# First batch of an attention and feed-forward kernel: scaling diagonals on GpSimd, value products on column halves, x split over all partitions

## The chip, the cores and the metric

The kernel runs on one core of one Trainium2 chip. A core has a matrix engine (TensorE, PE in the profile; its weight loads are listed apart as PEld), a vector engine (VectorE, DVE), a scalar engine (ScalarE, ACT), a general engine (GpSimd, POOL) and a queue engine that issues most transfers (SyncE, SP). The metric is device microseconds of one execution; the kernel before takes 1075.93 us (median of three runs, 1074.74 to 1076.09). A difference below about 0.2% can't be told from no change here.

## The reference

Eight batches of eight heads. Each head has 512 local rows and 32 global rows of 64 numbers. A local row attends to the 32 global keys and to the local keys no further than 32 rows away; a global row attends to everything. The concatenated heads (x, 512 wide, 544 rows a batch) go through a feed-forward layer.

```python
s_ll = np.where(np.abs(pos[:, None] - pos[None, :]) <= 32, scale * q_l @ k_l.T, -1e9)
s_l = np.concatenate([scale * q_l @ k_g.T, s_ll], axis=-1)
out_l = sm(s_l) @ np.concatenate([v_g, v_l])          # local rows
out_g = sm(scale * q_g @ k_all.T) @ v_all             # global rows
h = x @ w_in                                          # 512 x 2048
out = (np.maximum(h, 0) + np.log1p(np.exp(-abs(h)))) @ w_out
```

## The kernel before

Heads are taken in pairs: pair m is two heads of one batch, one on partitions 0 to 63 and one on 64 to 127. Pairs 0 to 3 are the first batch. They have code of their own (functions ending in 0), because nothing else can be done before x of the first batch is there. All later pairs run as small pieces (`scores`, `maxima`, `probs`, `values`, `combine`, `invert`, `normalise`) between the products of the feed-forward layer, which starts with batch 0.

The first batch is cut into eight local units (m, a), each two blocks of 128 query rows of both heads, so four row blocks a unit, and two global units (`scores0g` and so on), of two pairs each. A unit goes through seven stages, all in fp32:

- `scores0`: TensorE adds the mask and the products of queries and keys into PSUM (tile s, line 126 like every matmul); `soft0` takes the row maximum (VectorE, line 164), scales it (line 165), and ScalarE takes four exponentials with their sums (line 167).
- `invert0`: VectorE adds a small number to the sums and inverts them (lines 173 and 174).
- `diag0`: ScalarE multiplies the identity by the inverses, 128x128 for each of the four row blocks (line 181, tile diag). There are two diag tiles in turn.
- `turn0`: TensorE multiplies the exponentials by these diagonals, which transposes and normalises them in one step (tile t).
- `evict0`: ScalarE (line 208) and VectorE (line 209) copy t out of PSUM.
- `values0`: TensorE multiplies the values by them (tile o). Before, the stationary operand is 128 columns wide: both heads' values, so each product gives both heads' outputs against both heads' probabilities, and only the matching quarter blocks are used.
- `split0`: x is kept as a high part xh (ScalarE, line 226) and the remainder xl (VectorE, line 228), once for each head since the two heads' outputs stand in different columns.

The order is written out: a loop over k runs `scores0` of unit k + 2, the splitting of one weight block, `invert0` of unit k + 2, `values0` and `split0` of unit k - 2, `turn0` and `evict0` of unit k, and `diag0` of unit k + 2. Splitting a weight block takes, on each pass, one absolute value on ScalarE (line 479), four VectorE operations (lines 486, 488, 489, 492), a ScalarE cast (line 497) and a GpSimd subtraction (line 498). The helper `keep` ties each engine's operations of this part to that order. `diag0` comes before lines 497 and 479 on ScalarE. When the last units run, the pieces of pairs 4 and 5 begin, and after them the feed-forward products of batch 0 (tile h, then o from wo) with the remaining weight blocks; there no order is tied, and the scheduler's timeline sets each engine's order.

In each pass the later work of batch 0 needs xh and xl of all four pairs; the last is the xl of unit (3, 1). The global unit n = 1 has its scores in the PSUM tile oB, which the scores of unit (3, 1) used before it, so it waits for their exponentials.

Of the kernel before, what the change touches and what calls it, by code (L numbers as in the profile page):

```python
# [8 lines left out]
F32 = mybir.dt.float32  # L9
# [4 lines left out]
ALU = mybir.AluOpType  # L14
# [5 lines left out]
P = 128  # L20
# [33 lines left out]
def moe_over_global_local_attention(  # L54
# [12 lines left out]
    nc = tc.nc  # L67
# [3 lines left out]
    ps_h = ctx.enter_context(tc.tile_pool(name="ps_h", bufs=2, space=PSUM))  # L71
# [11 lines left out]
    identf = pl.tile([P, P], F32, tag="e", name="identf", bufs=2)  # L83
# [7 lines left out]
    for o, w, base, sign in ((32, 32, 0, 1), (64, 32, -96, -1), (96, 128, 32, 1), (96, 128, 32, -1)):  # L91
        r = mask0[:, 0, 1, o:o + w]
# [26 lines left out]
    def after(i, what):  # L119

        if what in order:
            tc.add_manual_dep(i.ins, order[what].name, mybir.DependencyInfo(mybir.DependencyClass.NoSync, mybir.DependencyReason.DATA), reason="order")
        return i

    def mm(*a, **k):
        order["pe"] = after(nc.tensor.matmul(*a, **k), "pe").ins  # L126
# [3 lines left out]
    st = {}  # L130
# [4 lines left out]
    xh, xl = {}, {}  # L135
# [14 lines left out]
    def keep(what, i):  # L150
        order[what] = after(i, what).ins
# [24 lines left out]
    def diag0(name, n):  # L176

        t = st.pop(("sums", name))
        d = st["diag", name] = pl.tile([P, 4, P], F32, tag="s2", name=f"diag{name}", bufs=2)
        for i in range(n):  # L180
            keep("act", nc.scalar.mul(d[:, i], identf, t[:, 0, i:i + 1]))

    def scores0(m, a):
        raw = st["raw0", m, a]
# [25 lines left out]

    def values0(m, a):
        t, vt = st.pop(("p0", m, a)), st["v0", m]
        ps = st["o0", m, a] = ps_h.tile([P, 512], F32, tag="h", name=f"o0_{m}_{a}").rearrange("p (c h q) -> p c h q", c=2, h=2)
        for c in range(2):
            for k, n in enumerate((P, 96)):
                mm(ps[:, c], lhsT=vt[:n, 2 * a + c, k], rhs=t[k][:n, :, c], start=k == 0, stop=k == 1, skip_group_check=True)

    def split0(m, a):
        ps = st.pop(("o0", m, a))
        if a == 0:  # L220
            xh[m] = pl.tile([P, 512], F32R, tag=f"xh{m}", name=f"xh0_{m}", bufs=1)
            xl[m] = pl.tile([P, 512], F32R, tag=f"xl{m}", name=f"xl0_{m}", bufs=1)
        hi, lo = ([x[m][r, 256 * a:256 * a + 256].rearrange("p (c q) -> p c q", c=2) for r in (slice(0, 64), slice(64, P))] for x in (xh, xl))
        part = [ps[64 * h:64 * h + 64, :, h] for h in range(2)]
        for h in range(2):
            keep("act", nc.scalar.copy(hi[h], part[h]))
        for h in range(2):
            keep("dve", nc.vector.tensor_tensor(lo[h], part[h], hi[h].bitcast(F32), op=ALU.subtract))  # L228


    def scores0g(n):
        ps = ps_s.tile([P, 2, 512], F32, tag=("oA", "oB")[n], name=f"s0g{n}")
# [249 lines left out]
    def bits_w(kind, k, a):  # L482
        t = raws.pop((kind, k))
        lo32, hi32 = t[:, :, 0], t[:, :, 1]

        i = nc.vector.tensor_scalar(a.bitcast(F32), a.bitcast(F32), TINY, None, op0=ALU.max)  # L486
        note("dve", i) if tight else after(i, "maxima")
        note("dve", nc.vector.tensor_scalar(a, a, 3, 0x3FFFFFFF, op0=ALU.logical_shift_left, op1=ALU.bitwise_and))
        note("dve", nc.vector.scalar_tensor_tensor(a, hi32, -0x40000000, a, op0=ALU.bitwise_and, op1=ALU.bitwise_or))  # L489

        r = lo32 if k < NF - 1 else pl.tile([P, 512], I32, tag="mb", name=f"wlast{kind}", bufs=2)
        note("dve", nc.vector.scalar_tensor_tensor(r, lo32, 29, a, op0=ALU.logical_shift_right, op1=ALU.bitwise_or))  # L492
        return r.bitcast(F32)
# [112 lines left out]
    i = order_w.index(("wi", NF - 1))  # L606
# [25 lines left out]
    first = end(H // 2 - 1) + 2 * STEP  # L632
    pcs = pieces()
    local = (scores0, lambda m, a: invert0((m, a), 4), lambda m, a: diag0((m, a), 4), turn0, evict0, values0, split0)
    glob = (scores0g, lambda n: invert0(n, 1), lambda n: diag0(n, 1), turn0g, evict0g, values0g, split0g)
    steps = [(local, (m, a)) for m in range(M0) for a in range(2)]
    for at, n in ((6, 0), (9, 1)):
        steps.insert(at, (glob, (n,)))
    n = len(steps)
# [6 lines left out]
    for k in range(-2, n + 2):  # L646
# [6 lines left out]
        if held:  # L653
            r = bits_w(*held)
# [91 lines left out]
```

## Time and profile before

| what | us |
|---|---|
| median of three timed runs | 1075.93 (1074.74 to 1076.09) |
| profiled execution, first to last instruction (its span; the page gives no other time of it) | 1072.0 |
| first product of the feed-forward layer starts | 90.80 |
| TensorE busy, whole span | 1014.0 (95%) |
| VectorE busy | 596.9 (56%) |
| ScalarE busy | 546.3 (51%) |
| GpSimd busy | 460.8 (43%) |

The share of busy time is an average. From 300 to 1000 us TensorE is busy over 99% of the time, and the other engines wait for it. In the first 200 us it has long gaps, and the question at each place is which engine the gap waits for. A row of a timeline has the start, the duration, the engine, the line, the operation, output<-input, the shape, and in brackets the idle time before it with what ended it.

### The profile page before, as it was taken

What the parts mean: (1) busy time and instruction counts of PE and PEld (TensorE: products, weight loads), DVE (VectorE), ACT (ScalarE), POOL (GpSimd) and SP (SyncE); (2) the same over time, 40 slices, a digit from 0 to 9 for tenths busy, and PEclk for the clock granted to TensorE, in tenths of its full rate; (3) what the DMA queues carried; (4) which work ended last, traced back from release to release, by engine and by line L of the source; (5) the groups of instructions that cost most, each with busy time, mean ns of one, the idle gap of its engine ahead of it and who ended that gap; (6) DMA issues with size and microseconds to landing.
All of it is one profiled execution on the core that took longest, in us unless ns stands there. A gap on an engine that the chain in (4) does not pass through costs nothing.

```text
span 1072.0 us, 14176 instructions
## 1 busy us (share of the span) xinstructions
PE 1014.0 (95%) x5108; PEld 801.9 (75%) x5108; DVE 596.9 (56%) x1138; ACT 546.3 (51%) x968; POOL 460.8 (43%) x526
## 2 busy tenths in 40 slices
PE   6895788899999999999999999999999999999996
PEld 4674566677777777777777777777777778888895
DVE  5978698976555655565555654565556542311211
ACT  6856555455445544545444544454444544554452
POOL 2226476653345444445444334544445541322321
PEclk9998899999999999999999999999999999999999
DMA  9523233313221312222221321231222210200000
GB/s 361 169 78 100 97 128 98 96 47 97 51 53 51 95 43 57 49 76 77 57 58 47 97 55 48 55 90 44 57 54 70 67 29 13 72 1 1 10 32 20
DMA packets 78565, 75.05 MB, mean 70 GB/s; under 512 B 53380, under 2 KB 57476, under 8 KB 78496
## 3 DMA queue, kind: packets, MB, share of 16 engines
q1 hardware_dynamic: 77952, 74.09, 23.5%
q8 instruction: 40, 0.66, 0.3%
q14 instruction: 29, 0.24, 0.1%
q10 hardware_dynamic: 544, 0.07, 0.0%
HBM read 64.43 MB, written 9.71 MB: 69 GB/s over the span
## 4 chain that ended last, share of the span: by engine, by line
PE 72%; DVE 10%; DMA 4%; issue 3%; POOL 1%; ACT 1%; SPq 0%; DVEq 0%; POOLq 0%; ACTq 0%
PE h L126 30%; PE o L126 29%; PE v_ps L126 8%; PE s_ps L126 5%; DMA rb<-rec_scratch 3%; DVE xa L404 2%; DVE xl L452 1%; DVE s L315 1%; DMA rec_scratch<-sc 1%; DVE wbitswo L489 1%; DVE xh L451 1%; DVE woraw L492 1%; DVE mb L347 0%; DVE e L543 0%; DVE wbitswo L486 0%
## 5 line engine op out<-in xcount | busy, mean ns | idle before, releaser
L126 PE MATMUL h<-xh,wi 128*128 128x512 f32 (+1 forms) x1152 | 356.4, 393 | 15.7 <-DVE xl L228 9.2
L126 PE MATMUL o<-wo,gh 128*128 128x512 f32 x1088 | 345.1, 398 | 0.0
L547 POOL TENSOR_TENSOR gl<-e,gh 128x512 fp32r<-128x512 f32 x136 | 177.3, 1304 | 386.4 <-ACT gh L546 318.2
L126 PEld LDWEIGHTS h<-xh,wi 128*128 128x128 f32 x1152 | 209.0, 190 | 62.8 <-issue 14.7
L126 PEld LDWEIGHTS o<-wo,gh 128*128 128x128 f32 x1088 | 199.9, 188 | 44.8 <-issue 5.2
L126 PE MATMUL h<-xl,wi 128*128 128x512 f32 (+1 forms) x576 | 220.3, 382 | 2.8 <-DVE xl L452 2.8
L126 PE MATMUL o<-wo,gl 128*128 128x512 f32 x544 | 213.4, 392 | 0.0
L540 ACT ACTIVATE e<-h 128x512 f32<-128x512 f32 x136 | 81.3, 598 | 240.1 <-PE h L126 238.6
L543 DVE SCALAR_TENSOR_TENSOR e<-h,e 128x512 f32<-128x512 f32 x136 | 93.2, 685 | 172.7 <-ACT e L542 167.7
L352 POOL TENSOR_TENSOR s<-s,mb 128x384 f32<-128x384 f32 x112 | 139.0, 1272 | 14.0 <-DVE mb L347 14.0
L546 ACT CAST gh<-e 128x512 fp32r<-128x512 f32 x136 | 83.9, 617 | 97.6 <-DVE e L543 97.5
L126 PEld LDWEIGHTS h<-xl,wi 128*128 128x128 f32 x576 | 109.4, 190 | 27.3 <-DVE xl L452 5.4
L126 PEld LDWEIGHTS o<-wo,gl 128*128 128x128 f32 x544 | 102.2, 188 | 22.8
L126 PE MATMUL v_ps<-s,v 128*65 128x192 f32 (+1 forms) x672 | 114.2, 313 | 4.2 <-DVE s L315 3.9
L126 PEld LDWEIGHTS v_ps<-s,v 128*65 128x65 f32 x672 | 88.5, 137 | 28.0 <-DVE s L315 5.9
L315 DVE TENSOR_TENSOR s<-s_ps,mask 128x768 f32<-128x768 f32 (+1 forms) x96 | 65.0, 696 | 76.6 <-PE s_ps L126 76.6
L356 ACT ACTIVATE s<-s 128x768 f32<-128x768 f32 (+1 forms) x84 | 66.5, 792 | 68.9 <-POOL s L352 45.6
L542 ACT ACTIVATE e<-e,one 128x512 f32<-128x512 f32 x136 | 98.3, 723 | 3.1
L126 PE MATMUL s_ps<-raw 64*128 64x192 f32 (+1 forms) x672 | 78.6, 347 | 14.0 <-issue 9.0
L541 ACT ACTIVATE e<-e 128x512 f32<-128x512 f32 x136 | 85.7, 630 | 3.6
L126 PEld LDWEIGHTS s_ps<-raw 64*128 64x128 f32 x672 | 53.3, 188 | 44.9 <-issue 33.4
L316 DVE TRANSPOSE_TENSOR_REDUCE mt<-s 128x24 f32<-128x768 f32 (+1 forms) x84 | 76.1, 907 | 10.7 <-ACT s L311 8.7
(144 smaller groups left out, 831.7 us busy)
## 6 DMA issues: line engine op xcount, KB each, us to landing
raw<-in_qk SPq DMA_DIRECT2D x56, 272.0 KB
v<-in_v SPq DMA_DIRECT2D x28, 384.0 KB
out<-ot SPq DMA_DIRECT2D x34, 256.0 KB
rb<-rec_scratch SPq DMA_DIRECT2D x28, 304.0 KB
wiraw<-in_w_in SPq DMA_DIRECT2D x16, 512.0 KB
woraw<-in_w_out SPq DMA_DIRECT2D x16, 512.0 KB
raw<-in_qk SPq DMA_DIRECT2D x28, 224.0 KB
v<-in_v SPq DMA_DIRECT2D x4, 512.0 KB
```

Source lines behind the costliest of these rows:

```text
L126: order["pe"] = after(nc.tensor.matmul(*a, **k), "pe").ins
L315: nc.vector.tensor_tensor(s[:, :, o:o + w], ps[:, :, o:o + w], mk.unsqueeze(1).to_broadcast([P, 2, w]), op=ALU.add)
L316: order["scores"] = nc.vector.tensor_reduce(windows(mt, 3 + 12 * p, 36, 2, nb), s.rearrange("p h (b k) -> p h b k", k=32), axis=AX.X, op=A ...
L352: nc.gpsimd.tensor_tensor(sw, sw, windows(mb[:, h], 0, 96, 2, 192), op=ALU.subtract)
L356: nc.scalar.activation(s, s, AF.Exp, scale=0.125)
L404: after(nc.vector.tensor_tensor(y[64 * h:64 * h + 64], x[0:64, h], rb[:, h], op=ALU.mult), "scores")
L540: nc.scalar.activation(e, ph, AF.Abs)
L541: nc.scalar.activation(e, e, AF.Exp, scale=-1.0)
L542: nc.scalar.activation(e, e, AF.Ln, bias=one)
L543: nc.vector.scalar_tensor_tensor(e, ph, 0.0, e, op0=ALU.max, op1=ALU.add)
L546: nc.scalar.copy(gh, e)
L547: nc.gpsimd.tensor_tensor(gl, e, gh.bitcast(F32), op=ALU.subtract)
```

## The change

Three edits in the functions of the first batch:

1. `diag0` makes all diagonals of a unit with one GpSimd multiplication, 128x512 for a local unit and 128x128 for a global one; both operands are read with broadcast patterns. The four ScalarE operations (one for a global unit) go. The GpSimd operation isn't tied to an order by `keep`.
2. `values0` makes a product for each head alone: the stationary operand is that head's 64 columns, the output goes to that head's 64 partitions. Eight products of 128 columns a unit in place of four of 256; the two heads' use different column halves of the array. The output tile takes 256 columns of a PSUM bank, with no unused blocks.
3. `split0` makes xh with one ScalarE operation over 128 partitions and xl with one VectorE operation, in place of two each over 64 partitions.

```diff
@@ diag0
-        for i in range(n):
-            keep("act", nc.scalar.mul(d[:, i], identf, t[:, 0, i:i + 1]))
+        nc.gpsimd.tensor_tensor(d[:, 0:n], identf.unsqueeze(1).to_broadcast([P, n, P]), t[:, 0, 0:n].unsqueeze(2).to_broadcast([P, n, P]), op=ALU.mult)
@@ values0
-        ps = st["o0", m, a] = ps_h.tile([P, 512], F32, tag="h", name=f"o0_{m}_{a}").rearrange("p (c h q) -> p c h q", c=2, h=2)
+        ps = st["o0", m, a] = ps_h.tile([P, 512], F32, tag="h", name=f"o0_{m}_{a}")[:, 0:256].rearrange("p (c q) -> p c q", c=2)
         for c in range(2):
             for k, n in enumerate((P, 96)):
-                mm(ps[:, c], lhsT=vt[:n, 2 * a + c, k], rhs=t[k][:n, :, c], start=k == 0, stop=k == 1, skip_group_check=True)
+                for h in range(2):
+                    r = slice(64 * h, 64 * h + 64)
+                    mm(ps[r, c], lhsT=vt[:n, 2 * a + c, k, r], rhs=t[k][:n, h, c], start=k == 0, stop=k == 1, skip_group_check=True)
@@ split0
-        hi, lo = ([x[m][r, 256 * a:256 * a + 256].rearrange("p (c q) -> p c q", c=2) for r in (slice(0, 64), slice(64, P))] for x in (xh, xl))
-        part = [ps[64 * h:64 * h + 64, :, h] for h in range(2)]
-        for h in range(2):
-            keep("act", nc.scalar.copy(hi[h], part[h]))
-        for h in range(2):
-            keep("dve", nc.vector.tensor_tensor(lo[h], part[h], hi[h].bitcast(F32), op=ALU.subtract))
+        hi, lo = (x[m][:, 256 * a:256 * a + 256].rearrange("p (c q) -> p c q", c=2) for x in (xh, xl))
+        keep("act", nc.scalar.copy(hi, ps))
+        keep("dve", nc.vector.tensor_tensor(lo, ps, hi.bitcast(F32), op=ALU.subtract))
```

The changed file is three lines shorter, so in the rows below line 498 of before is line 495 of the change, 492 is 489, 489 is 486, 543 is 540, and 374 and 375 are 371 and 372.

GpSimd's order in the passes of the first batch, before (wi and wo are weight blocks; each row is the subtraction that ends a block's splitting):

```order
L498 TENSOR_TENSOR wi_289<-wiraw_110,wi_289 128x512
L498 TENSOR_TENSOR wi_333<-wiraw_118,wi_333 128x512
L498 TENSOR_TENSOR wi_388<-wiraw_120,wi_388 128x512
L498 TENSOR_TENSOR wi_441<-wiraw_128,wi_441 128x512
L498 TENSOR_TENSOR wo_490<-woraw_130,wo_490 128x512
L498 TENSOR_TENSOR wo_543<-woraw_138,wo_543 128x512
```

The same place in the change (diag is the tile of the diagonals, with the unit behind it):

```order
L180 TENSOR_TENSOR diag(1, 0)_278<-identf,sums_0_216 128x512
L495 TENSOR_TENSOR wi_280<-wiraw_110,wi_280 128x512
L180 TENSOR_TENSOR diag(1, 1)_319<-identf,sums_1_293 128x512
L495 TENSOR_TENSOR wi_321<-wiraw_118,wi_321 128x512
L180 TENSOR_TENSOR diag(2, 0)_373<-identf,sums_0_334 128x512
L495 TENSOR_TENSOR wi_375<-wiraw_120,wi_375 128x512
L180 TENSOR_TENSOR diag(2, 1)_425<-identf,sums_1_388 128x512
L495 TENSOR_TENSOR wi_427<-wiraw_128,wi_427 128x512
L180 TENSOR_TENSOR diag_476<-identf,sumsg_440 128x128
L495 TENSOR_TENSOR wo_478<-woraw_130,wo_478 128x512
```

In every pass the weight subtraction now stands behind a diagonal.

VectorE's order at about 117 us of the profile before, where the feed-forward products run with the last weight blocks of the first stretch (x<-x,v_ps adds the overlap of two value products of pair 4 and frees their PSUM tile; e<-h frees a tile of the feed-forward layer):

```order
L489 SCALAR_TENSOR_TENSOR wbitswo_1141<-woraw_900,wbitswo_1141 128x512
L489 SCALAR_TENSOR_TENSOR wbitswi_1167<-wiraw_1009,wbitswi_1167 128x512
L374 TENSOR_TENSOR x_929<-x_929,v_ps_1_1032 65x2x64
L375 TENSOR_TENSOR x_929<-x_929,v_ps_1_1032 65x2x32
L492 SCALAR_TENSOR_TENSOR woraw_900<-woraw_900,wbitswo_1141 128x512
L543 SCALAR_TENSOR_TENSOR e_2_1000<-h_2_978,e_2_1000 128x512
L492 SCALAR_TENSOR_TENSOR wiraw_1009<-wiraw_1009,wbitswi_1167 128x512
```

The same place in the change:

```order
L486 SCALAR_TENSOR_TENSOR wbitswo_1133<-woraw_892,wbitswo_1133 128x512
L486 SCALAR_TENSOR_TENSOR wbitswi_1159<-wiraw_1001,wbitswi_1159 128x512
L489 SCALAR_TENSOR_TENSOR woraw_892<-woraw_892,wbitswo_1133 128x512
L489 SCALAR_TENSOR_TENSOR wiraw_1001<-wiraw_1001,wbitswi_1159 128x512
L371 TENSOR_TENSOR x_921<-x_921,v_ps_1_1024 65x2x64
L372 TENSOR_TENSOR x_921<-x_921,v_ps_1_1024 65x2x32
L540 SCALAR_TENSOR_TENSOR e_2_992<-h_2_970,e_2_992 128x512
```

Both last operations of the two weight blocks now stand ahead of the two additions. TensorE's order is the same in both but for the value products, and SyncE's is the same throughout.

## The prediction

> **What bounds the kernel now.** I read the windows by stage first (start and end, length, then busy us and instructions of PE, PEld, DVE, ACT, POOL, then granted clock, DMA share, GB/s), to see where TensorE is not the limit:
>
> ```profile
> 20.00:60.00 40.00, 36.30 (x213) 29.47 (x212) 34.34 (x70) 31.76 (x97) 9.09 (x7) 0.92 0.54 181
> 60.00:82.00 22.00, 21.58 (x159) 16.14 (x157) 17.69 (x34) 11.65 (x21) 8.29 (x10) 1.00 0.42 117
> 82.00:100.00 18.00, 7.69 (x27) 5.93 (x28) 15.03 (x29) 8.30 (x17) 11.76 (x15) 0.72 0.19 67
> 100.00:120.00 20.00, 11.99 (x58) 8.54 (x58) 19.76 (x25) 12.96 (x23) 11.05 (x8) 0.87 0.21 67
> ```
>
> GpSimd has 31 us free from 20 to 60; VectorE is full from 100 to 120. Then TensorE's timeline, for its gaps in these stages:
>
> ```profile
> 28.07 1.03 PE L126 MATMUL s<-raw 64*128 64x224 f32 x8
> 29.02 0.70 PE L126 MATMUL o<-p_1gh,v 128*128 128x256 f32 x2
> 31.50 2.03 PE L126 MATMUL t<-diag(1, 1)_328,e 128*128 128x128 f32 x16 [0.47 <-DVE p_0gl L209]
> 52.85 1.50 PE L126 MATMUL s0g<-raw,raw 128*128 128x256 f32 x4 [2.53 <-ACT e L167]
> 90.80 1.19 PE L126 MATMUL h<-xh,wi 128*128 128x512 f32 x2 [9.23 <-DVE xl L228]
> 119.61 1.01 PE L126 MATMUL s_ps<-raw 64*128 64x192 f32 x4 [4.59 <-issue]
> ```
>
> A pass of the first batch waits for VectorE (line 209); the scores of the second global unit for exponentials; the feed-forward layer for the last xl. From 60 to 82 us TensorE is busy 21.58 of 22. So the pass, not TensorE, sets the first 53 us. VectorE's timeline of one full pass:
>
> ```profile
> 29.59 0.16 DVE L173 TENSOR_SCALAR sums<-sums 128x4 f32<-128x4 f32 x1
> 29.79 0.18 DVE L174 RECIPROCAL sums<-sums 128x4 f32<-128x4 f32 x1
> 29.88 0.84 DVE L228 TENSOR_TENSOR xl<-o,xh 64x256 fp32r<-64x256 f32 x2
> 30.76 0.69 DVE L209 COPY p_0gl<-t 96x512 f32<-96x512 f32 x1
> 31.36 1.08 DVE L164 TENSOR_REDUCE sums<-s 128x4 f32<-128x896 f32 x1
> 32.48 0.74 DVE L165 TENSOR_SCALAR sums<-sums 128x4 f32<-128x4 f32 x1
> 33.13 0.41 DVE L486 TENSOR_SCALAR wbitswi<-wbitswi 128x512 f32<-128x512 f32 x1
> 33.58 0.43 DVE L488 TENSOR_SCALAR wbitswi<-wbitswi 128x512 int32<-128x512 int32 x1
> 34.04 0.69 DVE L489 SCALAR_TENSOR_TENSOR wbitswi<-wiraw,wbitswi 128x512 int32<-128x512 int32 x1
> 34.76 0.69 DVE L492 SCALAR_TENSOR_TENSOR wiraw<-wiraw,wbitswi 128x512 int32<-128x512 int32 x1
> 35.37 0.16 DVE L173 TENSOR_SCALAR sums<-sums 128x4 f32<-128x4 f32 x1
> 35.57 0.18 DVE L174 RECIPROCAL sums<-sums 128x4 f32<-128x4 f32 x1
> ```
>
> The pass takes 35.57 - 29.79 = 5.78 us and VectorE has no idle time in it. But line 165, 0.17 us where nothing is in its way, took 0.74: it ended when GpSimd's weight subtraction did.
>
> ```profile
> 31.89 1.30 POOL L498 TENSOR_TENSOR wi<-wiraw,wi 128x512 fp32r<-128x512 f32 x1 [4.41 <-ACT wi L497]
> ```
>
> 31.89 + 1.30 = 33.19. The reduction of line 164 ran beside the same subtraction at its usual length, so reads of PSUM pass and VectorE's operations on SBUF alone wait. Without that wait of 0.55 the pass would be 5.23. Other passes are longer (line 174 of each):
>
> ```profile
> 18.23 0.18 DVE L174 RECIPROCAL sums<-sums 128x4 f32<-128x4 f32 x1
> 41.76 0.16 DVE L174 RECIPROCAL sumsg<-sumsg 128x1 f32<-128x1 f32 x1
> 46.98 0.18 DVE L174 RECIPROCAL sums<-sums 128x4 f32<-128x4 f32 x1
> 53.24 0.18 DVE L174 RECIPROCAL sums<-sums 128x4 f32<-128x4 f32 x1
> ```
>
> The six from 18.23 to 53.24 average 5.84. Two rows show why:
>
> ```profile
> 26.71 1.05 DVE L486 TENSOR_SCALAR wbitswi<-wbitswi 128x512 f32<-128x512 f32 x1 [0.74 <-ACT wbitswi L479]
> 49.81 1.07 DVE L165 TENSOR_SCALAR sums<-sums 128x4 f32<-128x4 f32 x1
> ```
>
> Line 479 on ScalarE comes behind diag and the cast, and VectorE waits 0.74 for it; then line 486 is held 0.62 by the subtraction. At 49.81 the hold is 0.90.
>
> **The change, part by part.** The groups of lines with shapes kept apart (count, then busy us, mean ns):
>
> ```profile
> L498 POOL TENSOR_TENSOR wi<-wiraw,wi 128x512 fp32r<-128x512 f32 x9 | 12.2, 1352 | 43.7 <-ACT wi L497 39.7 <-issue 4.0
> L352 POOL TENSOR_TENSOR s<-s,mb 128x384 f32<-128x384 f32 x8 | 9.1, 1166 | 6.2 <-DVE mb L347 6.2
> L228 DVE TENSOR_TENSOR xl<-o,xh 64x256 fp32r<-64x256 f32 x16 | 6.7, 420 | 0.2
> L181 ACT ACTIVATE diag(2, 0)_383<-identf,sums 128x128 f32<-128x128 f32 x4 | 1.3, 388 | 0.4 <-DVE sums L174 0.4
> ```
>
> *Diagonals.* Removed: 1.28 us of ScalarE a pass, so lines 497 and 479 come that much earlier and VectorE's wait for 479 goes. Added: one GpSimd operation over 512 elements, not in the trace with broadcast reads. The nearest row is the subtraction of the same size, 1.30; from below the 384-element row bounds it (1.17), from above two subtractions (2.6). I take D = 1.30, since two-input operations of either layout (384 in windows, 512 in a row) cost some 2.5 to 3 ns an element. Queued behind it is the weight subtraction, whose hold on VectorE moves. Counting from line 174: diag starts at about 0.25 (the start of line 174, its 0.18, and a little for the signal) and ends at 0.25 + D. The subtraction is ready by then, since ScalarE no longer has diagonals ahead of the cast, and ends at 1.55 + D = 2.85.
>
> By a sentence of the Trainium skill (GPSIMD Engine Reference, Performance versus the Vector engine) a two-input operation takes about 2.6 cycles an element at 1.2 GHz, as an estimate 1.11 us for 512, and such work belongs on VectorE; by 1.11 the forecast would come about 1 us lower.
>
> *Split.* One xl of 0.42 in place of 0.84 a pass; twice the partitions of the same 256 elements (the copies over 96 and reductions over 128 partitions above show no price for partitions). ScalarE's halves save as much, under cover.
>
> The pass after: line 174, then xl at 0.09, 209 at 0.55, 164 at 1.15, 165 at 2.27, held until the subtraction ends at 2.85. From line 486 to the next 174 the rows above take 35.57 - 33.13 = 2.44. Together 1.55 + D + 2.44 = 5.29. Where the diagonal has 128 columns (the pass of 41.76), the subtraction is done by 1.9, nothing is held, and the pass is 2.27 + 0.10 + 2.44 = 4.81. ScalarE, busy 31.76 of 40 us before, loses some 1.6 us a pass and stays hidden.
>
> Up to 46.98 five passes took 28.75, now 4 x 5.29 + 4.81 = 25.97: 2.78 gained. In the last the exponentials of unit (3, 1) started 4.0 after line 174 (49.81 + 1.07 against 46.98), now 2.95: 1.05 more. So the global scores at 52.85 start **3.8 us earlier**. The passes before 18.23 I cost at nothing: the first two lose about 0.2 to a hold, the third gains it.
>
> *Value products.* Before, a unit's four take 2.0 us (29.02 to the end of the fourth pair). After, 16 instructions of 128 columns. The nearest row is the scores, products on row halves: 8 instructions of 224 columns in 1.03, 129 ns each; in proportion to columns 16 x 129 x 128/224 = 1.18, my lower bound. The t row, whole array, gives 2.03. Above that, if a half's weight load waits for the other half's product: 16 loads at 0.1 plus 2.03 is about 3.6 at the worst. I take 1.3, nearest the row on halves. In the passes this is cover only (scores 1.0 with mask 0.5, values 1.3, t 2.0: 4.8 of 5.29). On the path lies one group, of unit (2, 1), after the global scores and ahead of the gapless stretch: **0.7**.
>
> After 60 us the chain goes on through pair 4's scores, VectorE and GpSimd to the last xl; two xl there are shorter: **0.85**.
>
> *Moved.* In the scheduler's new order two line 492 operations stand ahead of the two additions that free a PSUM tile:
>
> ```profile
> 119.11 0.27 DVE L374 TENSOR_TENSOR x<-x,v_ps 65x128 f32<-65x128 f32 x1
> 119.31 0.20 DVE L375 TENSOR_TENSOR x<-x,v_ps 65x64 f32<-65x64 f32 x1
> 119.44 0.68 DVE L492 SCALAR_TENSOR_TENSOR woraw<-woraw,wbitswo 128x512 int32<-128x512 int32 x1
> ```
>
> TensorE's gap of 4.59 ends at 119.61, 0.10 after the second: behind a full VectorE that costs 2 x 0.68 = **1.36**. Other shifts in that stretch lie between the same waits; I cost them at nothing, and if they aren't hidden GpSimd's two subtractions now ahead of the first gl cost up to 2.6.
>
> Sum: 3.8 + 0.7 + 0.85 - 1.36 = 4.0. The profiled span becomes 1072.0 - 4.0 = 1068.0; with the 3.9 between span and median, **1071.9 us**. After 120 us nothing depends on absolute time: transfers are issued when buffers come free, so the shift is kept.
>
> **Rivals.** (a) *Slower: GpSimd's price.* The pass is D + 3.99, five passes count, so at D = 1.3 + 4.0/5 = 2.1 all is lost, and at 2.6 the time is 1075.9 + 2.5 = 1078.4. For it: broadcast reads are in no row. Against: both row layouts agree.
>
> (b) *The halves don't overlap.* With 2.0 for values TensorE's pass is 1.5 + 2.0 + 2.0 = 5.5, 0.2 over VectorE's in five passes, and the 0.7 is lost too: 1073.6. From 2.3 TensorE's pass is the 5.78 of before; at 3.6 it is 7.1, six passes lose 1.3 each against before and the group on the path 1.6, with 1.36 - 0.85 on top: 1086; at 2.8 some 1080. The row on halves speaks against the first. The Trainium skill (TensorE: Matmul & The Clock Gate, Part 3) says weight loads overlap running products only where the row groups differ, which column halves don't; it also lists a gain for column packing. No row here decides it.
>
> (c) *Lost later.* The gain arrives at 91 us, but the stretch to 120 is set by VectorE and GpSimd holding each other up (VectorE busy 19.76 of 20): 1.36 plus 2.6 unhidden leaves about 1.4, 1074.5.
>
> (d) *More.* The second global scores ran at a lower clock after their gap, from 52.85 to 56.57, the first from 33.37 to 35.46 (a window with its granted clock, 0.50, and three rows):
>
> ```profile
> 54.00:56.00 2.00, 2.00 (x7) 1.55 (x6) 0.59 (x2) 2.00 (x7) 0.18 (x1) 0.50 0.00 0
> ...
> 33.37 1.03 PE L126 MATMUL s0g<-raw,raw 128*128 128x256 f32 x4
> 35.46 0.68 PE L126 MATMUL o<-p_0gh,v 128*128 128x256 f32 x2
> 56.57 0.83 PE L126 MATMUL o<-p_1gh,v 128*128 128x256 f32 x2
> ```
>
> That is 3.72 against 2.09. If a shorter gap leaves the clock up, 1.6 more, and if the moves cost nothing, 1.36: 1068.9. Against it: TensorE's idle time within a pass grows by 0.7, which may lower the clock as well.
>
> **How the numbers follow.** Forecast 52%, (a) at 2.6 or more 9%, (b) light 6% and heavy 3%, (c) 16%, (d) 14%. The range, 1067.0 to 1077.5, holds (d) with D at its lower bound (5 x 0.13 = 0.7) and about as much again, the light (b), (c), and (a) up to D = 2.4. The forecast's own range is 1070 to 1074. Faster means under 1073.8 (0.2%, about what can be told from no change): the forecast, (d) and half of the light (b), 0.69. Same: (c) and the other half, 0.19. Slower, over 1078.1: (a) and the heavy (b), 0.12.
>
> **What would show it.** Right: diag rows near 1.3 on GpSimd with the subtraction straight behind; line 174 every 5.3 us; line 165 held about 0.6; value products near 1.3 a unit; xl single at 0.42; first h product at about 85.5 in place of 90.80; the gap ahead of 119.61 still ended by the additions. Wrong: diag over 2 us, TensorE without gaps before 45 us, or h early and the end not.

## The result and the profile after

The changed kernel takes 1069.93 us (median of four runs, 1067.27 to 1071.11), the kernel before 1076.01 beside it: a ratio of 0.9938 with a 95% interval of 0.9921 to 0.9955, so **faster**, by 6.1 us. The forecast was 1071.9. (Two executions among all those below were far longer, 2525.56 and 4940.62 us; the ratios leave them out.) The profiled execution of the change, the fastest of its four, ran from first to last instruction in 1065.1 us, 6.9 less than the one of before.

TensorE's timeline of the change, the rows that answer those shown of before (start, duration, and in brackets the idle time ahead with what ended it):

```profile
23.16 0.44 PE L126 MATMUL o<-p_0gh,v 128*64 128x128 f32 x4
...
23.87 0.39 PE L126 MATMUL o<-p_0gl,v 96*64 96x128 f32 x4
24.19 2.03 PE L126 MATMUL t<-diag(1, 0)_278,e 128*128 128x128 f32 x16
...
46.76 1.13 PE L126 MATMUL s0g<-raw,raw 128*128 128x256 f32 x4 [1.95 <-ACT e L167]
...
49.05 0.44 PE L126 MATMUL o<-p_1gh,v 128*64 128x128 f32 x4
...
82.80 1.19 PE L126 MATMUL h<-xh,wi 128*128 128x512 f32 x2 [10.69 <-DVE xl L226]
...
111.55 1.01 PE L126 MATMUL s_ps<-raw 64*128 64x192 f32 x4 [5.09 <-ACT wo L494]
```

The second global scores start 6.09 us earlier (52.85 to 46.76), the first feed-forward product 8.00 (90.80 to 82.80), the scores that end the next long gap 8.06 (119.61 to 111.55). The first two wait for what they waited for before, only earlier. The third row now names ScalarE (line 494) where before had “issue”; in both kernels the second of the two additions ends 0.10 ahead of the scores (119.31 + 0.20 against 119.61 before, 111.24 + 0.21 against 111.55 now). A unit's value products take 24.19 - 23.16 = 1.03 us in place of 2.0. The global scores take 49.05 - 46.76 = 2.29 in place of 3.72.

VectorE in the change, one full pass with the line 174 that ends it, and the line 174 of the first and the last pass counted below; then GpSimd in the same pass:

```profile
17.41 0.18 DVE L174 RECIPROCAL sums<-sums 128x4 f32<-128x4 f32 x1
...
27.46 0.18 DVE L174 RECIPROCAL sums<-sums 128x4 f32<-128x4 f32 x1
27.55 0.39 DVE L226 TENSOR_TENSOR xl<-o,xh 128x256 fp32r<-128x256 f32 x1
27.86 0.68 DVE L208 COPY p_0gl<-t 96x512 f32<-96x512 f32 x1
28.46 1.08 DVE L164 TENSOR_REDUCE sums<-s 128x4 f32<-128x896 f32 x1
29.57 0.53 DVE L165 TENSOR_SCALAR sums<-sums 128x4 f32<-128x4 f32 x1
30.02 0.42 DVE L483 TENSOR_SCALAR wbitswi<-wbitswi 128x512 f32<-128x512 f32 x1
...
32.56 0.18 DVE L174 RECIPROCAL sums<-sums 128x4 f32<-128x4 f32 x1
...
42.12 0.18 DVE L174 RECIPROCAL sums<-sums 128x4 f32<-128x4 f32 x1
```

```profile
27.78 1.04 POOL L180 TENSOR_TENSOR diag(2, 0)_373<-identf,sums 128x512 f32<-128x512 f32 x1 [2.71 <-DVE sums L174]
28.78 1.29 POOL L495 TENSOR_TENSOR wi<-wiraw,wi 128x512 fp32r<-128x512 f32 x1
```

The diagonals take 1.04 us, the subtraction stands straight behind them, and line 165 is held until it ends (28.78 + 1.29 = 30.07). The five passes from 17.41 to 42.12 take 24.71, where the same five took 28.75. The whole way from the first passes to the global scores is 0.82 (a pass of 3.72 in place of 4.52, up to 17.41 in place of 18.23) + 4.04 (these five) + 1.23 (line 174 to the scores, 4.64 in place of 5.87) = 6.09.

From 111.55 on the shift stays at about 8 us up to 237 us, and there 1.4 are lost at one place. Both kernels have two gaps there, 1.5 and 0.8 long. In the change the granted clock is half afterwards, in before it stays whole, as these windows show (start and end, length, busy us and instructions of PE, PEld, DVE, ACT and POOL, then granted clock, DMA share, GB/s; the change, then before):

```profile
233.20:236.61 3.41, 1.66 (x7) 0.72 (x5) 3.38 (x7) 1.90 (x3) 2.84 (x4) 1.00 0.36 90
236.61:240.02 3.41, 2.89 (x9) 2.09 (x10) 1.96 (x4) 1.33 (x3) 0.00 (x0) 0.50 0.40 150
```

```profile
241.21:244.62 3.41, 1.75 (x7) 0.81 (x5) 3.38 (x6) 1.75 (x3) 2.99 (x4) 1.00 0.35 87
244.62:248.03 3.41, 2.74 (x14) 2.29 (x15) 2.44 (x6) 2.38 (x5) 0.00 (x0) 1.00 0.41 154
```

The value products that follow the second gap show the price (the change, then before):

```profile
237.72 2.60 PE L126 MATMUL v_ps<-s,v 128*65 128x192 f32 x8
```

```profile
245.63 1.46 PE L126 MATMUL v_ps<-s,v 128*65 128x192 f32 x8
```

So the profile's 6.9 us are 6.1 by the global scores, 1.9 more by the first feed-forward product, about nothing (0.06) in the stretch behind it, and 1.2 given back behind that: 1.4 lost at 237 us, less 0.2 won elsewhere.

### The profile page after: what moved, and what is told of

Its sections match the earlier page's. It is cut to its first block, busy times and chain, and to the rows that moved or that the text cites. A ratio compares the mean times of both kernels' runs of the same rounds, so it can differ in the third digit from the quotient of the medians.

```text
span 1065.1 us, 14283 instructions
## 1 busy us (share of the span) xinstructions
PE 1008.1 (95%) x5172; PEld 798.0 (75%) x5172; DVE 592.5 (56%) x1130; ACT 533.2 (50%) x926; POOL 469.1 (44%) x536
## 4 chain that ended last, share of the span: by engine, by line
PE 72%; DVE 10%; DMA 4%; issue 3%; POOL 1%; ACT 1%; SPq 0%; DVEq 0%; POOLq 0%; ACTq 0%
PE h L126 30%; PE o L126 29%; PE v_ps L126 8%; PE s_ps L126 5%; DMA rb<-rec_scratch 2%; DVE xa L401 2%; DVE xl L449 1%; DVE s L312 1%; DMA rec_scratch<-sc 1%; DVE wbitswo L486 1%; DVE xh L448 1%; DVE wbitswi L483 1%; DVE wbitswo L483 1%; DVE mb L344 0%; DVE woraw L489 0%
## 5 line engine op out<-in xcount | busy, mean ns | idle before, releaser
L126 PE MATMUL h<-xh,wi 128*128 128x512 f32 (+1 forms) x1152 | 357.6, 394 | 15.2 <-DVE xl L226 10.7
```

## The experiments

Two theories stood against each other. The **theory of the passes**: VectorE's pass became shorter, because the diagonals left ScalarE and so the weight subtraction comes earlier and holds VectorE less; value products and the split add a little. The **theory of the clock**: the second global scores happened to run at full clock, and that is a large part of it. Beside them stood the question what each of the three edits is worth. All ratios below are to the kernel before on the same chip, with 95% intervals.

**The change once more.** The same kernel, in a second session.

> The changed kernel once more, to set the others of this group against it on the same chip. Both theories: 1068 to 1071 us, 5 to 7 us under the kernel before. What is open is its profile: the theory of the passes (the gain is the shorter pass of VectorE, D + 3.99 with the measured D of 1.04, plus shorter value products and one operation for xl) expects again line 174 every 5.0 us and the second global scores at 46.8; the theory of the clock (the second global scores ran at full clock by luck, 2.29 us in place of 3.72) expects that a second profile may show them at 3.7 again and the first h product 1.4 later, at about 84.2.

1068.48 us, 0.9944 (0.9922 to 0.9965). Its profile repeats the first: line 174 every 5.02 us, global scores at 46.77 and at full clock, first feed-forward product at 82.54. On the clock it decides nothing: the points at which the granted clock can change (see the last section) stood nearly where they stood in the first profile, at 1.17 modulo 3.41 us against 1.09.

**The diagonals alone.** In the kernel before:

```diff
-        for i in range(n):
-            keep("act", nc.scalar.mul(d[:, i], identf, t[:, 0, i:i + 1]))
+        nc.gpsimd.tensor_tensor(d[:, 0:n], identf.unsqueeze(1).to_broadcast([P, n, P]), t[:, 0, 0:n].unsqueeze(2).to_broadcast([P, n, P]), op=ALU.mult)
```

> The kernel before with the GpSimd diagonals alone. Theory of the passes: counted from line 174, the two xl end at 0.93, line 165 could start at 2.65, and the subtraction ends at 0.25 + 1.04 + 1.30 = 2.59, so nothing is held and VectorE's pass is 2.65 + 0.10 + 2.44 = 5.2; TensorE's own work in a pass is then 1.5 + 2.0 + 2.0 = 5.5 and sets it. Five passes gain 0.3 to 0.6 each, with the 0.8 after the last of them 2.3 to 3.8 us in all: 1072 to 1074 us. Theory of the clock: with TensorE nearly gapless in the passes the second global scores run at full clock and 1.4 more is gained, 1071 us. If the diagonals alone give the whole 6 us, the value products and the split were worth nothing.

1068.30 us, 0.9939 (0.9920 to 0.9958): the whole gain, and 3 to 6 us under what I gave. A row of VectorE, one of GpSimd in the same pass, and one of TensorE:

```profile
30.28 0.17 DVE L165 TENSOR_SCALAR sums<-sums 128x4 f32<-128x4 f32 x1
```

```profile
28.89 1.30 POOL L497 TENSOR_TENSOR wi<-wiraw,wi 128x512 fp32r<-128x512 f32 x1
```

```profile
48.04 1.13 PE L126 MATMUL s0g<-raw,raw 128*128 128x256 f32 x4 [0.84 <-ACT e L167]
```

The subtraction ends at 30.19, line 165 starts at 30.28 and is not held: VectorE's own work sets the pass, 5.35 here, 5.02 to 5.36 in all. My figure of 5.2 for this was near; that TensorE's 5.5 would set the pass was wrong. The scores start at 48.04, 1.3 later than with all three edits, and the gap ahead of them is only 0.84. They run at full clock.

**Value products and split without the GpSimd diagonals.** The reverse edit, in the change:

```diff
-        nc.gpsimd.tensor_tensor(d[:, 0:n], identf.unsqueeze(1).to_broadcast([P, n, P]), t[:, 0, 0:n].unsqueeze(2).to_broadcast([P, n, P]), op=ALU.mult)
+        for i in range(n):
+            keep("act", nc.scalar.mul(d[:, i], identf, t[:, 0, i:i + 1]))
```

> The change without the GpSimd diagonals: they stay on ScalarE; value products on column halves and one split operation. Theory of the passes: the shorter xl (0.42 less) ends in the hold, because line 165 still waits for the subtraction, which still stands behind the diagonals and the cast; the pass stays between 5.4 (ScalarE's shorter split lets the cast come 0.4 earlier) and 5.8. On the path remain one group of value products (1.0 measured in place of 2.0) and two xl (0.85): 1.8 gained at 5.8, 3.7 at 5.4, so 1072 to 1074 us. Theory that the diagonals do nothing by themselves: 1070, as the whole change.

1071.16 us, 0.9960 (0.9947 to 0.9973), a little under my 1072 to 1074. The first three full passes are 5.78, 5.87 and 5.76, as before. VectorE in the third of them:

```profile
31.97 0.17 DVE L165 TENSOR_SCALAR sums<-sums 128x4 f32<-128x4 f32 x1
32.50 1.08 DVE L484 TENSOR_SCALAR wbitswi<-wbitswi 128x512 f32<-128x512 f32 x1 [0.36 <-ACT wbitswi L477]
```

The time that the shorter xl leaves goes into a wait for ScalarE (0.36) and into the hold by the subtraction (1.08 in place of 0.42). The theory of the passes had it all in the hold, and on line 165. Still the scores start at 50.66, 2.2 earlier than before, since the two passes around the first global unit (6.19 became 5.71, 5.22 became 4.89) and the last aren't bound that way. By the ratios the two halves of the change are worth 0.6% and 0.4%, and the whole 0.6%: they don't add up. The rows say the same:

```profile
86.62 1.19 PE L126 MATMUL h<-xh,wi 128*128 128x512 f32 x2 [10.62 <-DVE xl L227]
```

The first feed-forward product comes 4.18 earlier than before with these two edits, 6.50 (84.30) with the diagonals alone, and 8.00 with all three.

**The split in two operations again**, in the change:

```diff
-        hi, lo = (x[m][:, 256 * a:256 * a + 256].rearrange("p (c q) -> p c q", c=2) for x in (xh, xl))
-        keep("act", nc.scalar.copy(hi, ps))
-        keep("dve", nc.vector.tensor_tensor(lo, ps, hi.bitcast(F32), op=ALU.subtract))
+        hi, lo = ([x[m][r, 256 * a:256 * a + 256].rearrange("p (c q) -> p c q", c=2) for r in (slice(0, 64), slice(64, P))] for x in (xh, xl))
+        part = [ps[64 * h:64 * h + 64] for h in range(2)]
+        for h in range(2):
+            keep("act", nc.scalar.copy(hi[h], part[h]))
+        for h in range(2):
+            keep("dve", nc.vector.tensor_tensor(lo[h], part[h], hi[h].bitcast(F32), op=ALU.subtract))
```

> The change with the split in two operations of 64 partitions each again, for xh on ScalarE and xl on VectorE (0.42 each). Theory of the passes: in the passes the second xl fills time in which line 165 is held anyway (held 0.5 to 0.9 in the change), so line 174 stays at 5.0 us; only the two xl of the last chain to the first h product count, 0.85, and the two ScalarE halves ahead of them, some 0.8 at most: h 0.8 to 1.7 later than 82.80, time 1071 to 1071.7 us. If instead every pass loses 0.42, the second global scores start 2.1 later and the time is 1073.

1070.69 us, 0.9948 (0.9929 to 0.9967), within the interval of the change. I expected the second xl to vanish in the hold; it did not:

```profile
28.44 0.86 DVE L229 TENSOR_TENSOR xl<-o,xh 64x256 fp32r<-64x256 f32 x2
...
31.05 0.17 DVE L165 TENSOR_SCALAR sums<-sums 128x4 f32<-128x4 f32 x1
31.13 0.42 DVE L486 TENSOR_SCALAR wbitswi<-wbitswi 128x512 f32<-128x512 f32 x1
```

The hold beyond line 165's own 0.17 was 0.36, and VectorE became more than that later (0.47 of xl, and xl starts 0.22 after line 174 in place of 0.09). Line 486 starts 31.13 - 28.22 = 2.91 after line 174 (at 28.22), against 30.02 - 27.46 = 2.56 with one operation, and the four passes from there on are 5.36, 5.05, 5.21 and 5.35, together 20.97. With the diagonals alone these four take 20.96, with the whole change 19.69. So what shortens the passes beyond the diagonals is the split, by 1.3 us in four of them, and the value products add nothing there. The profiled execution was the longest of this kernel's (1073.68): one pass ahead of these took 5.78, and the clock was half from 48.0 to 54.9, so its rows behind 48 us are not compared.

**The diagonals twice**: the GpSimd line stands twice, and writes the same result again.

```diff
         nc.gpsimd.tensor_tensor(d[:, 0:n], identf.unsqueeze(1).to_broadcast([P, n, P]), t[:, 0, 0:n].unsqueeze(2).to_broadcast([P, n, P]), op=ALU.mult)
+        nc.gpsimd.tensor_tensor(d[:, 0:n], identf.unsqueeze(1).to_broadcast([P, n, P]), t[:, 0, 0:n].unsqueeze(2).to_broadcast([P, n, P]), op=ALU.mult)
```

> The change with every GpSimd diagonal made twice in a row (the same result, written again), so that its price D is 2.08 in place of 1.04. Theory of the passes: pass = D + 3.99, so line 174 every 6.07 us, line 165 held about 1.6 in each pass, five passes 1.04 longer: the second global scores 5.2 later, at about 52.0, and the time 5.2 up, about 1075 us, and 1076.5 if their clock falls as well. Rival: GpSimd's price is hidden (31 us free between 20 and 60 us), and the time stays within 1 us of the change, 1070.

1074.10 us, 0.9989 (0.9976 to 1.0003): nearly all the gain is gone. GpSimd and VectorE in one pass:

```profile
29.88 1.04 POOL L180 TENSOR_TENSOR diag(2, 0)_377<-identf,sums 128x512 f32<-128x512 f32 x1 [2.17 <-DVE sums L174]
30.88 1.29 POOL L496 TENSOR_TENSOR wi<-wiraw,wi 128x512 fp32r<-128x512 f32 x1
32.13 1.29 POOL L181 TENSOR_TENSOR diag(2, 0)_377<-identf,sums 128x512 f32<-128x512 f32 x1
```

```profile
31.67 0.53 DVE L165 TENSOR_SCALAR sums<-sums 128x4 f32<-128x4 f32 x1
32.11 0.41 DVE L484 TENSOR_SCALAR wbitswi<-wbitswi 128x512 f32<-128x512 f32 x1
32.56 1.15 DVE L486 TENSOR_SCALAR wbitswi<-wbitswi 128x512 int32<-128x512 int32 x1
```

The scheduler put the second one behind the subtraction, so the hold fell on line 486 (1.15 in place of 0.43), and the pass is 5.71, 0.69 longer, in place of the 6.07 that I gave for a D of 2.08. Five passes later the scores start at 50.22, 3.46 after the change's, and the clock halved there; first feed-forward product 87.79. That GpSimd is idle for most of a pass does not hide its price: here each operation is paid through what it holds on VectorE.

**The diagonals on VectorE**, one operation in the same place:

```diff
-        nc.gpsimd.tensor_tensor(d[:, 0:n], identf.unsqueeze(1).to_broadcast([P, n, P]), t[:, 0, 0:n].unsqueeze(2).to_broadcast([P, n, P]), op=ALU.mult)
+        keep("dve", nc.vector.tensor_tensor(d[:, 0:n], identf.unsqueeze(1).to_broadcast([P, n, P]), t[:, 0, 0:n].unsqueeze(2).to_broadcast([P, n, P]), op=ALU.mult))
```

> The change with the diagonals on VectorE, one operation a unit, in the same place of the order. No row shows this operation on VectorE; a two-input operation of 128x512 fp32 there takes 0.69 (line 489's row). By the theory of the passes GpSimd's subtraction is then done at about 0.25 + 0.69 + 1.3 = 2.2 or sooner and holds nothing, but VectorE's own work is 0.69 longer: 0.69 + 2.27 + 0.10 + 2.44 = 5.5 a pass, 0.47 longer than with GpSimd in five passes: 2.3 up, about 1072 us. The rule of the Trainium skill (GPSIMD Engine Reference, Performance versus the Vector engine) that such elementwise work belongs on VectorE expects at least no loss: 1070 or under.

1077.28 us, 1.0008 (0.9990 to 1.0026): the gain is gone, and far more than the 2.3 that I expected. The global scores start at 53.31, 6.55 after the change's, and at half clock. VectorE and GpSimd:

```profile
30.30 1.80 DVE L180 TENSOR_TENSOR diag(2, 0)_373<-identf,sums 128x512 f32<-128x512 f32 x1
```

```profile
30.25 1.30 POOL L495 TENSOR_TENSOR wi<-wiraw,wi 128x512 fp32r<-128x512 f32 x1 [3.63 <-ACT wi L494]
```

In five of the eight local units the operation takes 0.67 to 0.69, as the estimate had it, and a pass with such a one was 5.45. In the other three it takes 1.80: the subtraction shown started 0.05 sooner, VectorE waited for it, and that pass is 6.37. The Trainium skill (SBUF — State Buffer, Who interferes with whom) says that a VectorE operation with two SBUF inputs and a GpSimd operation that reads SBUF contend for one shared pair of ports, that this is an exclusive lock, and that the order of issue decides which of them waits. These two rows agree: 1.80 is 1.11 more than 0.69, and the subtraction took 1.30. The rule of the Trainium skill that elementwise work belongs on VectorE (GPSIMD Engine Reference, Performance versus the Vector engine) would have lost the whole gain here, since VectorE is the engine that sets the pass.

**Another tile for the second global scores.** In the change, so that they don't wait for the exponentials of unit (3, 1):

```diff
-        ps = ps_s.tile([P, 2, 512], F32, tag=("oA", "oB")[n], name=f"s0g{n}")
+        ps = ps_s.tile([P, 2, 512], F32, tag="oA", name=f"s0g{n}")
```

> The change with the second global scores in the PSUM tile oA in place of oB, which the scores of unit (3, 1) hold until their exponentials are done. Theory of the passes: TensorE's gap of 1.95 us ahead of 46.76 goes nearly whole, since oA is free by then, and what follows it on TensorE comes up to 1.9 earlier; the chain to the first h product passes through it: h at 81 in place of 82.80, time 1068 to 1069. Rival: the value products and turns behind it wait for the same exponentials and normalisations anyway, so the gap only moves behind the global scores: 1070.

1066.74 us, 0.9921 (0.9902 to 0.9939). I had given 1068 to 1069. The gap is gone, and the gain arrives:

```profile
44.76 1.13 PE L126 MATMUL s0g<-raw,raw 128*128 128x256 f32 x4
...
80.72 1.19 PE L126 MATMUL h<-xh,wi 128*128 128x512 f32 x2 [10.62 <-DVE xl L226]
```

**The same once more**, beside the two below:

> The change with the second global scores in tile oA once more, beside the three others on the same chip: 1066 to 1068 us if the first result holds, global scores at 44.8 and full clock there wherever the grid stands, since no gap is left to halve it.

1066.25 us, 0.9911 (0.9895 to 0.9928), scores at 44.73, first feed-forward product at 80.42. This is the best kernel of the study, 9 us under before.

**That tile alone**, the same edit in the kernel before:

> The kernel before, with the second global scores in the PSUM tile oA as the only edit. If gaps and clock at this place are worth what the run with the change showed (1.95 us gap gone, 2.0 earlier), here the gap of 2.53 goes: these scores at 50.3 in place of 52.85 and at full clock (1.4 more where the clock fell): 2.5 to 3.9 us gained, about 1072.4 us, with the passes at 5.78 as before. Rival: in the old passes the work behind these scores waits for the same exponentials, the gap moves, 1075.5.

1070.77 us, 0.9952 (0.9934 to 0.9971): by itself about 5 us, with all passes as long as before.

```profile
50.22 1.13 PE L126 MATMUL s0g<-raw,raw 128*128 128x256 f32 x4
...
87.46 1.19 PE L126 MATMUL h<-xh,wi 128*128 128x512 f32 x2 [9.23 <-DVE xl L228]
```

The scores start 2.63 earlier and run at full clock, and the first feed-forward product comes 3.34 earlier. The span of this profile, 1071.9, doesn't show the gain: the profiled execution was the longest of its seven (1074.03), and behind 140 us it has four stretches at half clock where the profile of before has two.

**The diagonals and that tile**, without value products and split:

> The kernel before with the GpSimd diagonals and tile oA for the second global scores, without the value products on column halves and without the split in one operation. With no gap there the clock stays up in either version, so what is left of the difference to the change with oA is those two edits. Theory of the passes: passes of 5.02 to 5.36 as with the diagonals alone, global scores at about 47.2 (44.76 with all three), h at 83.5 (80.72), of which some 0.7 is made up by 148 us as with the diagonals alone: 1068.5, against 1066.7. Rival: the diagonals are the whole gain, and the time is 1066.7 as well.

1070.93 us, 0.9951 (0.9933 to 0.9969): 4.7 more than all edits with that tile on the same chip, where I expected 1.8.

```profile
46.52 1.13 PE L126 MATMUL s0g<-raw,raw 128*128 128x256 f32 x4
...
82.78 1.19 PE L126 MATMUL h<-xh,wi 128*128 128x512 f32 x2 [9.22 <-DVE xl L227]
...
112.92 1.01 PE L126 MATMUL s_ps<-raw 64*128 64x192 f32 x4 [2.44 <-issue]
```

The first feed-forward product is 2.36 later than with all edits, and in the stretch behind it another 2.3 go (scores after the gap at 112.92 against 108.29), where VectorE's order is the scheduler's. So the value products and the split together were worth nothing against the diagonals alone with the old tile (1068.30 against 1068.48) and 4.7 with the new one. The tile, in turn, gave about 5 us in the kernel before, some 2 to 3 on top of all three edits, and nothing that can be told on top of the diagonals alone (0.9951 against 0.9939, on another chip). What each of these edits is worth by itself stays open. That it depends on an order which shifts with every edit is likely and was not shown.

**The kernel before once more**, for a second profile:

> The kernel before once more, for a second profile of it. In the profiles so far the granted clock changes only at points a whole multiple of 3.41 us apart, and a stretch of 3.41 at half clock follows one in which TensorE was busy under about half. Theory of the grid: the grid stands elsewhere against the kernel in this execution (it stood at 2.27 modulo 3.41 in the first profile of before); the 2.53 us gap ahead of the second global scores halves the clock only if 1.7 us of idle time fall into one stretch, that is for 2.5 of 3.41 positions, 74 in 100, and else these scores take 2.3 in place of 3.72 with nothing changed in the kernel. Rival: the gap's length alone decides, so they take 3.7 again wherever the grid stands.

1076.47 us, 1.0003 (0.9990 to 1.0016). It doesn't tell the two expectations apart: the points at which the clock can change stood nearly in the same place (2.49 modulo 3.41, against 2.27, with the kernel's rows 0.46 later), and the scores took 3.7 again. So it is known from the rows of single profiles what the clock was worth at this place, but not how much of it is in the medians.

**The last xl earlier in the order.** In the change, each turn of the loop emits value products and split of unit k - 2 ahead of the pieces of pairs 4 and 5:

```diff
         stage(k + 2, 0)
+        stage(k - 2, 5)
+        stage(k - 2, 6)
...
         stage(k + 2, 1)
-        stage(k - 2, 5)
-        stage(k - 2, 6)
         stage(k, 3)
```

> The change with the value products and the split of unit k - 2 ahead of the pieces of pairs 4 and 5 in each turn of the last passes, so that xl of unit (3, 1) isn't behind them. It tests that the gap of 10.69 us ahead of the first h product (82.80) is set by the place of that xl in the order and not by its inputs. If so, h starts 3 to 8 us earlier; as the time behind h was kept from there on, 1 to 5 us are gained, 1065 to 1069 us. Rival: the work that fills TensorE before the gap now stands behind h's start, the sum of TensorE's work ahead of the steady stretch is unchanged and the gap moves: 1070, or some us more where a piece of pair 4 comes late.

1077.55 us, 1.0013 (0.9995 to 1.0030), where I had given 1065 to 1069. The edit was broader than my words: it also put xl ahead of the weight bits and `invert0` in every pass, and three passes took 7.67, 7.97 and 6.99. The scores start at 55.24. What it tells is in the stretch behind:

```profile
86.53 1.22 PE L126 MATMUL h<-xh,wi 128*128 128x512 f32 x2 [3.51 <-DVE xl L226]
...
121.28 1.01 PE L126 MATMUL s_ps<-raw 64*128 64x192 f32 x4 [3.15 <-issue]
```

From the scores to the first feed-forward product it takes 31.3 us in place of 36.0, with a gap of 3.5 in place of 10.7, and from there to the scores after the gap 34.8 in place of 28.8. The 4.7 gained are given back and 1.2 more, so in this order the long gap ahead of that product only changes place. Since the edit was so broad, it doesn't show that a narrower one would do the same.

## Why the prediction was right, point by point

- **The number.** The measured 1069.93 lies inside the range, 2.0 under the forecast and 1.0 over rival (d), just below the 1070 to 1074 that the forecast had for its own. What bounds the kernel, the diagonals as the largest part, and the way of the change were right; that the sum came so near was partly luck, as the terms below show.
- **What bounds.** Right: VectorE's pass sets the first 50 us. Doubling GpSimd's diagonals or putting them on VectorE lengthens the passes and takes the gain, with TensorE's work as it was. (In both of these profiles the clock at the second global scores was half as well.)
- **Diagonals.** The formula held, the price in it did not. The pass is D + 3.99, and with the measured D of 1.04 that is 5.03; measured 5.02, 5.03, 5.10 and 4.92, and 4.64 for the short one (forecast 4.81). I took D = 1.30 from a subtraction of the same size, and even my lower bound of 1.17 lay too high: a row with contiguous operands did not bound one with broadcast ones. The estimate of 1.11 from the Trainium skill's sentence would have been nearer. Five passes gained 4.04 in place of 2.78.
- **The first passes** I costed at nothing; they gained 0.82, as line 174 of the third pass comes earlier: before, VectorE waited there 0.71 for line 479, which stood behind the diagonals on ScalarE. With the diagonals alone it comes at 17.41 too, with the other two edits alone at 18.21. The last pass gained 1.23 against 1.05. Together the global scores came 6.09 earlier, not 3.8.
- **Value products 0.7 and split 0.85** behind the scores: neither term added up as I had it. With the clock full in both, from the scores to the first feed-forward product it takes 82.80 - 46.76 = 36.04 with all three edits and 84.30 - 48.04 = 36.26 with the diagonals alone: 0.2, not 1.55. Without the GpSimd diagonals it takes 86.62 - 50.66 = 35.96, also at full clock. Of the 1.91 that this stretch became shorter (37.95 before), 0.7 goes to the clock (37.24 with the other tile alone, 87.46 - 50.22, whose scores run at full clock). The other 1.2 come with the diagonals alone (1.0) nearly as well as with these two edits alone (1.3): by these rows either saves the same time, and the second adds next to nothing. So my 1.55 was near for the two edits by themselves, and wrong as a term beside the diagonals. TensorE's gain of 1.0 a unit stands beside a longer gap (10.69 after 9.23). With the other tile it is 36.26 against 35.69 and 35.96, 0.3 to 0.6. The split counts in the passes, 1.3 us in four of them.
- **Moved operations, -1.36:** wrong, nothing was lost. From the first feed-forward product to the scores after the gap, 28.75 in place of 28.81. The two line 489 operations do stand ahead of the additions there, and VectorE runs without idle time from line 486 to the additions; which of its holds earlier in the stretch went in return stays open:

```profile
108.64 0.68 DVE L486 SCALAR_TENSOR_TENSOR wbitswo<-woraw,wbitswo 128x512 int32<-128x512 int32 x1
...
110.44 0.68 DVE L489 SCALAR_TENSOR_TENSOR wiraw<-wiraw,wbitswi 128x512 int32<-128x512 int32 x1
111.04 0.27 DVE L371 TENSOR_TENSOR x<-x,v_ps 65x128 f32<-65x128 f32 x1
```

  Here, where two engines hold each other up, an operation that moved ahead didn't cost its length.
- **3.9 between span and median:** an execution lies about 2 us over its span (1067.27 against 1065.1 for the change; 1078.20 against 1076.2 for before), so the profiled execution of before took about 1074.1 by this estimate, below its median; the other 1.8 us of my term is spread between runs.
- **Rivals.** (a) fell, at D = 1.04. That more GpSimd work lengthens the pass is real, but the diagonals run twice showed 0.69 a pass for 1.29 of work behind the subtraction, not one for one as the formula has it. (b) fell: 16 products of 128 columns on column halves take 1.03 us, 64 ns each, where the 16 of the t row, on the whole array, take 2.03. The Trainium skill (TensorE: Matmul & The Clock Gate, Part 3) ties the overlap of weight loads to different row groups, and lists a gain for column packing. Here the row groups are the same, and the gain came. Whether one half's load overlaps the other half's product, or a load of 64 columns is only shorter, these rows don't tell. (c) happened neither in the stretch to 120 us nor by its mechanism, though 1.4 are lost at 237. (d) came true in both halves in the profile, 1.43 of clock at the scores (of which 0.7 was left by the first feed-forward product) and 1.36 of moves; the sum came within 2.0 of the median because the gains that I undersized met the terms that didn't add and the loss at 237. The first half of (d) is partly luck and not the change's own: with nearly the same gap, the clock stayed up in the change and fell with the diagonals run twice (see the last section).

## What to carry to other kernels

An idle engine is not a free one: one GpSimd operation of 1.3 us more in each pass cost VectorE 0.7, and with the measured price of that operation the formula that counted the hold gave the change's passes to 0.2 us; for the doubled operation it was 0.36 too high. Before operations are made shorter, look for a tile that makes an engine wait for the wrong thing: another tile for one stage gave 5 us by itself, though not beside every other edit. And a gain computed on an engine that then has a gap is no gain: ask where the gap's end is set.

## What the runs showed of the hardware

**The clock goes by a grid.** In all fourteen profiles, from 40 to 260 us, the granted clock changes only at points a whole multiple of 3.41 us apart, and where these stand differs between executions (0.3 to 3.3 modulo 3.41; five of the fourteen near 1.1). Of the 89 falls from full to half clock there, 82 stand behind a stretch in which TensorE was busy for under half. The two pairs of windows that show it best are those with nearly the same gap; first the diagonals twice, gap 1.92, then the change, gap 1.95:

```profile
47.67:51.08 3.41, 1.49 (x9) 1.02 (x8) 3.27 (x6) 2.58 (x10) 1.80 (x2) 1.00 0.00 0
51.08:54.50 3.42, 3.42 (x16) 2.91 (x16) 1.38 (x6) 1.22 (x2) 2.85 (x3) 0.50 0.00 0
```

```profile
45.47:48.88 3.41, 2.12 (x12) 1.91 (x12) 2.25 (x7) 3.13 (x10) 1.41 (x2) 1.00 0.00 0
48.88:52.29 3.41, 3.41 (x37) 3.05 (x38) 2.93 (x6) 1.21 (x4) 0.88 (x1) 1.00 0.00 0
```

In the first the gap fell into one stretch (1.49 of 3.41 busy, 44%) and the next ran at 0.50. In the second the gap was cut in two by the grid (62%), and the clock stayed. The windows at 233.20 and 241.21 above show the same near the edge: busy 1.66 of 3.41 (49%) halved it, 1.75 (51%) did not. One stretch of another profile (value products and split without the GpSimd diagonals, from 48.63) was busy 47% by this count and kept the clock, so the bound is only about half. And the busy share is not the whole rule: seven falls stand behind a stretch that was busy for 50 to 81%. In six of them that stretch ends in the long gap ahead of the first feed-forward product, and products of 64 columns run in it, in the change too:

```profile
69.36:72.77 3.41, 2.75 (x20) 2.41 (x20) 2.79 (x5) 0.84 (x1) 3.18 (x4) 1.00 0.93 299
72.77:76.19 3.42, 0.00 (x0) 0.00 (x0) 1.10 (x5) 2.25 (x5) 2.98 (x7) 0.50 0.92 359
```

Why the clock fell there stays open. The Trainium skill (TensorE: Matmul & The Clock Gate, Part 1) has the free-running window of 3.41 us; it speaks of an idle window, and here one that is half idle was enough. So a gap of 2 us costs more or nothing, by where it falls; up to 1.7, as an estimate, since a stretch of 3.41 at half clock does the work of half its length. That this makes up part of the 3 to 9 us between runs of one kernel is likely but was not shown: only profiled executions have a clock by time.

**A multiplication with broadcast operands was cheaper on GpSimd than a subtraction of the same size**: 1.04 against 1.29 for 128x512 fp32, in all eight local units, and 0.40 for 128x128. The same multiplication issued behind the subtraction took 1.22 to 1.29 in five units of six, beside VectorE operations, and 1.04 in the sixth; whether it waits for them was not tried. So whether the operation, its operands or what ran beside it makes the difference of 0.25 is open.
